# One core, attention into two expert layers: v rows for block means load into the place of the second batch's keys; norm's factor, key slices and the spread of w_out's conversion change with it

## The chip, the core and the metric

The kernel runs on one core of a Trainium2 chip. The metric is the time of one execution on the device in microseconds (us), median of the runs. Engines are named as in the profile: PE (TensorE), PEld (its weight loads), DVE (VectorE), ACT (ScalarE), POOL (GpSimd), SP (SyncE, which issues all DMAs here). L154 is line 154 of the kernel before.

## The reference

Attention with a local window and block summaries, then two feed-forward layers. Float32 throughout; the four weight matrices of the two layers arrive as float64.

```python
k_sum = k.reshape(B, H, nb, block, D).max(axis=3)      # B=2 H=8 S=768 D=64 block=32
v_sum = v.reshape(B, H, nb, block, D).mean(axis=3)
scores_l = scale * q @ k.T                             # only |i - j| < 16 kept
scores_s = scale * q @ k_sum.T + log(block)
a = softmax(concat(scores_l, scores_s))                # max subtracted
x = a @ concat(v, v_sum)                               # 1536 tokens x 512
h = x @ w_in                                           # 512 -> 1024
solu = h * softmax(h)
ln = (solu - mean) / sqrt(var + 1e-6) * g_ln
x = ln @ w_out                                         # 1024 -> 512
h = x @ w_in2                                          # 512 -> 2048
out = where(h > 0, h, exp(min(h, 0)) - 1) @ w_out2     # 2048 -> 512
```

## The kernel before, in words

**Attention.** The 1,536 tokens are cut into 24 units of 64 queries, 12 per batch. Unit n takes a window of 96 keys and the 24 block maxima of its batch: `attn_s` (L168) makes a tile kw of 120 keys by copying a slice of k_sb on POOL (L176) and, in the first units of a batch, the maxima ksum (L175), multiplies it with a block-diagonal q (s_ps, L179), masks on DVE (L185), takes exp on ACT (L188) and divides on POOL (L193). `attn_p` transposes the result (p_ps, L198), `attn_x` multiplies it with a tile vw of 96 rows of v and 24 block means (x_ps, L215); ACT writes the high part of xT (L218), DVE the remainder (L219, shown as L95). kw and vw have three buffers each, k_sb two places (one per batch), q four.

**Block means.** `sum_v` (L150) loads 768 rows of v in six DMAs (L154), and PE multiplies them with an averaging matrix (vs_ps, L156). The rows go into `v_rows`: parts of the tiles y1 and y2, which are free until the first layer's output is written. The same parts are `stage`, the places into which the 64-bit words of w_in are loaded: words 0 and 1 go into y0, 2 and 3 into the part of y1 where the v rows lie, 4 and 5 into y2, 6 and 7 into y0 again.

**Weights.** `convert` (L106) loads 512 KB of words (L107) and makes two float32 numbers of each float64, a high part and a remainder: ACT takes the absolute value (L113), POOL clamps (L114), DVE does three bit operations (L115 to L117), for w_out POOL multiplies with norm's factor g (L119), ACT copies the high part (L120), DVE subtracts (L121, shown as L95). Each product of the two layers is three matmuls on these parts (`mm3x`, L97 to L100).

**First layer.** Row tile j of 128 tokens needs units 2j and 2j+1. h is computed for two halves n of w_in, then `ffn1_ln` does the norm on DVE, ACT and POOL (L230 to L244), `ffn1_tr` transposes it on PE (t_ps, L254) and splits it into lnT on ACT and DVE (L256, L257), and `mm_out` multiplies three row tiles at once with w_out (y_ps). **Second layer.** Three blocks of 512 tokens, with w_in2 and w_out2 converted by `load_w3` and `load_w4` as the work goes on.

**What sets the order.** The order on SP is written by hand (`manual_schedule`, L352): a prologue (L354 to L384), then 24 ticks (L398), of which each loads, computes half a row tile of h, and does one step of the attention of units 3, 4 and 6 ticks ahead, with transposes (`after`), conversions (`converts`, L396) and w_in2 loads (L421) at fixed ticks. A DMA on SP waits for the DMA eight places earlier, and for the readers of the place into which it loads. The order of the other engines comes from the scheduler, and each engine works strictly in its order.

Of the kernel before, what the change touches and what calls it, by code (L numbers as in the profile page):

```python
# [9 lines left out]
F32 = mybir.dt.float32  # L10
# [4 lines left out]
AF = mybir.ActivationFunctionType  # L15
# [7 lines left out]
TQ = 64  # L23
# [11 lines left out]
NEG = -1.0e9  # L35
LEAD = 6
NBUF = 3
NG = 6


# [9 lines left out]
def tile_kernel(ctx: ExitStack, tc: tile.TileContext, qd, kT, v, w_in, w_out, g_ln, w_in2, w_out2,  # L50
# [10 lines left out]

    y = [com.tile([128, KD, TC], F32, name=f"y{i}") for i in range(NTOK // TC)]
    flat = [t.rearrange("p d s -> p (d s)") for t in y]
    rows = [[t[:, i * DM:(i + 1) * DM] for i in range(KD * TC // DM)] for t in flat]
    stage = [[t.bitcast(I32)[:, i * 1024:(i + 1) * 1024].rearrange("p (k f) -> p k f", k=KD)
              for i in range(KD * TC // 1024)] for t in flat]

# [14 lines left out]
    negh = p_ln.tile([128, 1], F32, name="negh")  # L82
    dump = p_ln.tile([128, F1], BF16, name="dump")
    mask = p_at.tile([128, 3, KW], F32, name="mask", bufs=1)
    kws = [p_at.tile([128, NP, KW], F32, name=f"kw{i}", bufs=1) for i in range(NBUF)]
    vws = [p_at.tile([128, DM], F32, name=f"vw{i}", bufs=1) for i in range(NBUF)]
    avg = p_at.tile([128, 128 + NB], F32, name="avg", bufs=1)
    nc.gpsimd.memset(negh, -0.5)
# [17 lines left out]
    def convert(bits, src, hi, lo, g=None):  # L106
        nc.sync.dma_start(bits, src if len(src.shape) == 3 else src.rearrange("p (k f) -> p k f", k=KD))  # L107
        words = bits.rearrange("p k (f two) -> p k f two", two=2)
        low, high = words[:, :, :, 0], words[:, :, :, 1]
        hi, lo = (t if len(t.shape) == 3 else t.rearrange("p (k f) -> p k f", k=KD) for t in (hi, lo))  # L110
        a = p_k.tile([128, KD, 128], I32, tag="conv", name="conv", bufs=3)
        x = a.bitcast(F32)
        nc.scalar.activation(x, high.bitcast(F32), AF.Abs)  # L113
        nc.gpsimd.tensor_scalar(x, x, F64_HUGE, F64_TINY, op0=ALU.min, op1=ALU.max)  # L114
        nc.vector.tensor_scalar(a, a, 3, 0x3FFFFFF8, op0=ALU.logical_shift_left, op1=ALU.bitwise_and)  # L115
        nc.vector.scalar_tensor_tensor(a, high, -0x40000000, a, op0=ALU.bitwise_and, op1=ALU.bitwise_or)
        nc.vector.scalar_tensor_tensor(a, low, 29, a, op0=ALU.logical_shift_right, op1=ALU.bitwise_or)  # L117
        if g is not None:
            nc.gpsimd.tensor_scalar(x, x, g, 0.0, op0=ALU.mult, op1=ALU.add)  # L119
        nc.scalar.activation(hi, x, AF.Copy)  # L120
        lo_of(lo, x, hi)  # L121

    early = stage[0] + stage[1] + stage[2]
    v_rows = rows[1] + rows[2]

    def load_w_in(n, k):
        cs = slice(n * 512, (n + 1) * 512)
# [21 lines left out]

    def sum_v(b):  # L150
        pst = psb.tile([128, DM], F32, tag="b", name="vs_ps")
        for i in range(S // 128):
            vt = v_rows[i]
            nc.sync.dma_start(vt, v[b, PAD + i * 128:PAD + (i + 1) * 128, :])  # L154
            c0 = NB - i * 4
            nc.tensor.matmul(pst, lhsT=avg[:, c0:c0 + 128], rhs=vt, start=i == 0, stop=i == S // 128 - 1)  # L156
        vsum[b] = p_at.tile([128, DM], F32, tag="vsum", name="vsum", bufs=1)
        nc.scalar.activation(vsum[b][WIN:KW, :], pst[WIN:KW, :], AF.Copy)
# [5 lines left out]
    def load_v(n):  # L164
        b, t = divmod(n, NT)
        nc.sync.dma_start(vws[n % NBUF][0:WIN, :], v[b, t * TQ:t * TQ + WIN, :])

    def attn_s(n):  # L168
        b, t = divmod(n, NT)
        j, half = divmod(n, 2)  # L170
        kw = kws[n % NBUF]
        if n not in q_bd:
            load_q(n)
        if t < NBUF and n:
            copy_pool(kw[:, :, WIN:KW], ksum[b])  # L175
        copy_pool(kw[:, :, 0:WIN], k_sb[b][:, :, t * TQ:t * TQ + WIN])  # L176
        sps = psb.tile([128, NP, 128], F32, tag="b", name="s_ps")
        for p in range(NP):
            nc.tensor.matmul(sps[:, p, 0:KW], lhsT=q_bd[n][:, p, :], rhs=kw[:, p, :], start=True, stop=True)  # L179
        sm = p_at.tile([128, NP, KW], F32, tag="sm", name="sm", bufs=NBUF)  # L180
        st = p_at.tile([128, 4, NP], F32, tag="st", name="st", bufs=NBUF)
        nm, ss, ri = (st[:, i, :] for i in range(3))
        mi = 1 if t == 0 else (2 if t == NT - 1 else 0)
        for p in range(NP):
            nc.vector.tensor_tensor_reduce(sm[:, p, :], sps[:, p, 0:KW], mask[:, mi, :], -scale, 3.0e38,  # L185
                                           op0=ALU.add, op1=ALU.min, accum_out=nm[:, p:p + 1])
        for p in range(NP):
            nc.scalar.activation(sm[:, p, :], sm[:, p, :], AF.Exp, bias=nm[:, p:p + 1], scale=-1.0,  # L188
                                 accum_out=ss[:, p:p + 1])
        nc.vector.tensor_scalar(ri, ss, 1e-9, None, op0=ALU.add)  # L190
        nc.vector.reciprocal(ri, ri)  # L191
        for p in range(NP):
            nc.gpsimd.tensor_scalar(sm[:, p, :], sm[:, p, :], ri[:, p:p + 1], 1.0, op0=ALU.mult, op1=ALU.mult)  # L193
        live[n] = sm
# [198 lines left out]
    for i, t in ((0, 11), (1, 17)):  # L393
        for d in range(KD):
            after[t + d].append((mm_out, i, d))
    converts = {3: 2, 4: 1, 6: 1, 9: 2, 10: 2}  # L396
    NU = B * NT
    for t, (j, n) in enumerate(ticks):  # L398
        s_n, p_n, x_n = t + LEAD, t + LEAD - 2, t + LEAD - 3
        if t == 0:  # L400
            sum_v(1)
        elif t == 1:
            load_k(1)
        elif t == 3:
            sum_k(1)
        if x_n < NU and t:
            load_v(x_n)
        if s_n < NU:
            for u in (s_n + 1, s_n):
                if u < NU and u not in q_bd:  # L410
                    load_q(u)
            attn_s(s_n)
        mm_in(j, n)
        if p_n < NU:
            attn_p(p_n)
        for f, *args in after[t]:
            f(*args)
        if x_n < NU:
            attn_x(x_n)
        more(converts.get(t, 0))  # L420
        if t in (13, 15, 17, 18, 19, 20, 21, 22):  # L421
            load_w3()
        if x_n == NU - 1:
            p_at.release()
            p_w3 = ctx.enter_context(tc.tile_pool(name="p_w3", bufs=1, side="left", reuse_waits="tile"))
            lnT_last = [p_w3.tile([128, KF1, TB], F32R, tag=f"lnT{c}", name="lnT") for c in range(2)]
# [35 lines left out]
             f == 0, f == KF2 - 1)  # L462

    def store(i, ops, t):
        o = rows[0][t]
        r0 = i * TC + t * 128
        if i == NTOK // TC - 1 and t == NTT - 1:
            for c in range(2):
                cs = slice(c * 256, (c + 1) * 256)
                if c:  # L470
                    nc.vector.tensor_copy(o[:, cs], ops[t][:, cs])
                else:
                    nc.scalar.activation(o[:, cs], ops[t][:, cs], AF.Copy)
                nc.sync.dma_start(out[r0:r0 + 128, cs], o[:, cs])
            return
        if t % 2:
            nc.vector.tensor_copy(o, ops[t])
        else:
            nc.scalar.activation(o, ops[t], AF.Copy)
        nc.sync.dma_start(out[r0:r0 + 128, :], o)  # L480
# [77 lines left out]
```

## Time and profile before

| | |
|---|---|
| median of 3 runs | 510.34 us (509.59 to 511.14) |
| profiled execution | 507.9 us |
| its span | 505.8 us |
| mean granted clock of PE | 0.993 |
| busy in the span | PE 96%, DVE 56%, ACT 52%, POOL 26% |

The shares are means over the whole span. PE's busy time counts matmuls at whatever clock they ran, and a matmul may wait inside a busy stretch, so the stages have to be read apart: in which of them does PE stand still, who releases it, and at what clock does it run behind that?

### The profile page before, as it was taken

The page shows a single profiled execution, that of the slowest core. Times are in us where ns is not written, and L with a number is a line of the kernel's source. Part 1 is how long each engine was busy: PE and PEld are TensorE (multiplying, and loading weights), DVE is VectorE, ACT ScalarE, POOL GpSimd, SP SyncE. Part 2 cuts the span into 40 slices and gives each one's busy share as a digit, 9 for nine tenths or more (in the row PEclk, how much of TensorE's full clock was granted, in tenths as well). Part 3 has the DMA queues.
Part 4 walks back from the last instruction along what each step waited for, and adds up shares of the span by engine and source line. Part 5 has one row for each costly group of instructions (what it writes and reads, how often), then busy time and mean ns, then how long its engine had stood idle before and what let it go on. Part 6 is the DMA issues. An engine that isn't in the chain of part 4 may idle for free.

```text
span 505.8 us, 7269 instructions
## 1 busy us (share of the span) xinstructions
PE 483.2 (96%) x2616; PEld 400.5 (79%) x2616; DVE 283.5 (56%) x680; ACT 261.8 (52%) x592; POOL 131.0 (26%) x216
## 2 busy tenths in 40 slices
PE   1789997999999999999999999999999999999997
PEld 1466876888988888999888888888888888888885
DVE  3689799798458747797999622351222235122222
ACT  1675896776568436655767433352323335232333
POOL 1867688688413321322232100000000000000000
PEclk9999998999999999999999999999999999999999
DMA  8989473171313400565454000020000002000002
GB/s 302 286 296 311 132 231 120 38 233 39 115 59 116 141 1 0 208 172 166 155 173 126 1 0 0 1 84 1 1 1 0 0 1 84 1 0 0 1 0 83
DMA packets 24563, 46.53 MB, mean 92 GB/s; under 512 B 2256, under 2 KB 11088, under 8 KB 24528
## 3 DMA queue, kind: packets, MB, share of 16 engines
q1 hardware_dynamic: 24528, 46.08, 28.6%
q8 instruction: 20, 0.33, 0.3%
q14 instruction: 15, 0.12, 0.1%
HBM read 42.93 MB, written 3.15 MB: 91 GB/s over the span
## 4 chain that ended last, share of the span: by engine, by line
PE 88%; DMA 3%; DVE 3%; ACT 2%; POOL 1%; issue 1%; SPq 1%; ACTq 0%; POOLq 0%
PE h L98 13%; PE h L100 13%; PE h L99 13%; PE o_ps L98 9%; PE o_ps L99 9%; PE o_ps L100 9%; PE y_ps L98 5%; PE y_ps L100 4%; PE s_ps L179 4%; PE y_ps L99 4%; PE x_ps L215 2%; DMA q_bd<-in_qd 2%; PE p_ps L198 2%; PE t_ps L254 1%; DMA k_sb<-in_kT 1%
## 5 line engine op out<-in xcount | busy, mean ns | idle before, releaser
L454 DVE SCALAR_TENSOR_TENSOR m<-m,h 128x512 f32<-128x512 f32 x48 | 32.9, 685 | 120.0 <-ACT m L453 119.8
L452 ACT ACTIVATE m<-h 128x512 f32<-128x512 f32 x48 | 28.7, 598 | 107.5 <-PE h L100 107.2
L99 PE MATMUL h<-y_hl,w 128*128 128x512 f32 x192 | 75.9, 395 | 0.0
L100 PE MATMUL h<-y_hl,w 128*128 128x512 f32 x192 | 75.9, 395 | 0.0
L98 PE MATMUL o_ps<-w,g_hl 128*128 128x512 f32 x192 | 75.5, 393 | 0.0
L99 PE MATMUL o_ps<-w,g_hl 128*128 128x512 f32 x192 | 75.4, 393 | 0.0
L98 PE MATMUL h<-y_hl,w 128*128 128x512 f32 x192 | 75.2, 395 | 0.0
L100 PE MATMUL o_ps<-w,g_hl 128*128 128x512 f32 x192 | 66.9, 392 | 0.0
L114 POOL TENSOR_SCALAR conv<-conv 128x512 f32<-128x512 f32 x48 | 36.4, 761 | 67.2 <-ACT conv L113 65.9
L193 POOL TENSOR_SCALAR sm<-sm,st 128x120 f32<-128x120 f32 x96 | 44.9, 484 | 16.7 <-DVE st L191 15.8
L95 DVE TENSOR_TENSOR g_hl<-m,g_hl 128x512 fp32r<-128x512 f32 x48 | 33.9, 707 | 24.4 <-ACT g_hl L455 24.4
L455 ACT ACTIVATE g_hl<-m 128x512 fp32r<-128x512 f32 x48 | 30.3, 630 | 32.5 <-DVE m L454 32.5
L179 PE MATMUL s_ps<-kw,q_bd 128*128 128x120 f32 x192 | 29.6, 301 | 15.9 <-DMA q_bd<-in_qd 13.3
L98 PE MATMUL y_ps<-lnT,w_out 128*128 128x384 f32 x128 | 44.0, 344 | 0.3 <-DVE lnT L95 0.2
L100 PE MATMUL y_ps<-lnT,w_out 128*128 128x384 f32 x128 | 43.1, 338 | 0.0
L99 PE MATMUL y_ps<-lnT,w_out 128*128 128x384 f32 x128 | 43.1, 336 | 0.0
L99 PEld LDWEIGHTS h<-y_hl,w 128*128 128x128 f32 x192 | 36.1, 188 | 8.6
L98 PEld LDWEIGHTS o_ps<-w,g_hl 128*128 128x128 f32 x192 | 36.1, 188 | 8.5
L100 PEld LDWEIGHTS h<-y_hl,w 128*128 128x128 f32 x192 | 36.1, 188 | 8.5
L98 PEld LDWEIGHTS h<-y_hl,w 128*128 128x128 f32 x192 | 36.1, 188 | 8.5
L100 PEld LDWEIGHTS o_ps<-w,g_hl 128*128 128x128 f32 x192 | 36.1, 188 | 8.2
L99 PEld LDWEIGHTS o_ps<-w,g_hl 128*128 128x128 f32 x192 | 36.1, 188 | 8.2
(77 smaller groups left out, 913.1 us busy)
## 6 DMA issues: line engine op xcount, KB each, us to landing
y<-in_w_in SPq DMA_DIRECT2D x20, 512.0 KB, 4.6
y<-in_w_out SPq DMA_DIRECT2D x16, 512.0 KB, 4.3
q_bd<-in_qd SPq DMA_DIRECT2D x24, 256.0 KB, 5.0
vw<-in_v SPq DMA_DIRECT2D x24, 192.0 KB, 4.2
bits<-in_w_out SPq DMA_DIRECT2D x8, 512.0 KB, 3.5
k_sb<-in_kT SPq DMA_DIRECT2D x8, 400.0 KB, 5.5
y<-in_v SPq DMA_DIRECT2D x12, 256.0 KB, 5.4
out<-y SPq DMA_DIRECT2D x11, 256.0 KB, 2.3
```

The costliest lines, as they stand in the source:

```text
L95: nc.vector.tensor_tensor(out_, x, hi.bitcast(F32), op=ALU.subtract)
L98: nc.tensor.matmul(ps, lhsT=l[0][ls], rhs=r[0][rs], start=first, stop=False)
L99: nc.tensor.matmul(ps, lhsT=l[0][ls], rhs=r[1][rs], start=False, stop=False)
L100: nc.tensor.matmul(ps, lhsT=l[1][ls], rhs=r[0][rs], start=False, stop=last)
L114: nc.gpsimd.tensor_scalar(x, x, F64_HUGE, F64_TINY, op0=ALU.min, op1=ALU.max)
L179: nc.tensor.matmul(sps[:, p, 0:KW], lhsT=q_bd[n][:, p, :], rhs=kw[:, p, :], start=True, stop=True)
L193: nc.gpsimd.tensor_scalar(sm[:, p, :], sm[:, p, :], ri[:, p:p + 1], 1.0, op0=ALU.mult, op1=ALU.mult)
L198: nc.tensor.transpose(pps[:KW, p, :], live[n][:, p, :], ident)
L215: nc.tensor.matmul(xps[ds, p, :], lhsT=vw[:KW, p * 128 + hh * D:p * 128 + (hh + 1) * D], rhs=pT[:KW, p, hh * TQ:(hh + 1) * TQ], start=True ...
L452: nc.scalar.activation(m, h2, AF.Relu, scale=-1.0)
L454: nc.vector.scalar_tensor_tensor(m, m, -1.0, h2, op0=ALU.add, op1=ALU.max)
L455: nc.scalar.activation(gh, m, AF.Copy)
```

## The change

- **v rows.** `sum_v` allocates a tile v_sb with tag "k" of pool p_k, which has two places. For batch 0 that is the place that k_sb of batch 1 will have. v_sb of batch 0, v_sb of batch 1 and then k_sb of batch 1 use it one after the other. y1 and y2 hold only words of weights until the first layer's output.
- **Norm's factor.** In `convert` for w_out, POOL's multiplication is gone. ACT's copy multiplies with g, and DVE computes x*g - hi in one operation.
- **Key slices.** kw has four buffers. Units 12 to 23 load their 96 keys from memory with a DMA of 192 KB (128 partitions, 4 pieces of 384 bytes), issued in the tick before; units 0 to 11 copy on POOL as before.
- **Spread of w_out's conversions.** One in each of the ticks 3 to 10, not 2, 1, 1, 2, 2 in the ticks 3, 4, 6, 9, 10. Seven w_in2 loads stand in the ticks of the first layer, not eight.

```diff
--- before.py
+++ after.py
@@ -35,6 +35,8 @@
 NEG = -1.0e9
 LEAD = 6
 NBUF = 3
+NKW = 4
+NCOPY = 12
 NG = 6
 
 
@@ -61,7 +63,7 @@
 
     y = [com.tile([128, KD, TC], F32, name=f"y{i}") for i in range(NTOK // TC)]
     flat = [t.rearrange("p d s -> p (d s)") for t in y]
-    rows = [[t[:, i * DM:(i + 1) * DM] for i in range(KD * TC // DM)] for t in flat]
+    rows = [t[:, i * DM:(i + 1) * DM] for t in flat[:1] for i in range(KD)]
     stage = [[t.bitcast(I32)[:, i * 1024:(i + 1) * 1024].rearrange("p (k f) -> p k f", k=KD)
               for i in range(KD * TC // 1024)] for t in flat]
 
@@ -82,7 +84,7 @@
     negh = p_ln.tile([128, 1], F32, name="negh")
     dump = p_ln.tile([128, F1], BF16, name="dump")
     mask = p_at.tile([128, 3, KW], F32, name="mask", bufs=1)
-    kws = [p_at.tile([128, NP, KW], F32, name=f"kw{i}", bufs=1) for i in range(NBUF)]
+    kws = [p_at.tile([128, NP, KW], F32, name=f"kw{i}", bufs=1) for i in range(NKW)]
     vws = [p_at.tile([128, DM], F32, name=f"vw{i}", bufs=1) for i in range(NBUF)]
     avg = p_at.tile([128, 128 + NB], F32, name="avg", bufs=1)
     nc.gpsimd.memset(negh, -0.5)
@@ -115,13 +117,14 @@
         nc.vector.tensor_scalar(a, a, 3, 0x3FFFFFF8, op0=ALU.logical_shift_left, op1=ALU.bitwise_and)
         nc.vector.scalar_tensor_tensor(a, high, -0x40000000, a, op0=ALU.bitwise_and, op1=ALU.bitwise_or)
         nc.vector.scalar_tensor_tensor(a, low, 29, a, op0=ALU.logical_shift_right, op1=ALU.bitwise_or)
-        if g is not None:
-            nc.gpsimd.tensor_scalar(x, x, g, 0.0, op0=ALU.mult, op1=ALU.add)
-        nc.scalar.activation(hi, x, AF.Copy)
-        lo_of(lo, x, hi)
+        if g is None:
+            nc.scalar.activation(hi, x, AF.Copy)
+            lo_of(lo, x, hi)
+        else:
+            nc.scalar.activation(hi, x, AF.Copy, scale=g)
+            nc.vector.scalar_tensor_tensor(lo, x, g, hi.bitcast(F32), op0=ALU.mult, op1=ALU.subtract)
 
     early = stage[0] + stage[1] + stage[2]
-    v_rows = rows[1] + rows[2]
 
     def load_w_in(n, k):
         cs = slice(n * 512, (n + 1) * 512)
@@ -149,8 +152,9 @@
 
     def sum_v(b):
         pst = psb.tile([128, DM], F32, tag="b", name="vs_ps")
+        v_sb = p_k.tile([128, NP, S + 2 * PAD], F32, tag="k", name="v_sb", bufs=2).rearrange("p a s -> p (a s)")
         for i in range(S // 128):
-            vt = v_rows[i]
+            vt = v_sb[:, i * DM:(i + 1) * DM]
             nc.sync.dma_start(vt, v[b, PAD + i * 128:PAD + (i + 1) * 128, :])
             c0 = NB - i * 4
             nc.tensor.matmul(pst, lhsT=avg[:, c0:c0 + 128], rhs=vt, start=i == 0, stop=i == S // 128 - 1)
@@ -165,15 +169,22 @@
         b, t = divmod(n, NT)
         nc.sync.dma_start(vws[n % NBUF][0:WIN, :], v[b, t * TQ:t * TQ + WIN, :])
 
+    def load_kw(n):
+        b, t = divmod(n, NT)
+        if NCOPY <= n < B * NT:
+            nc.sync.dma_start(kws[n % NKW][:, :, 0:WIN],
+                              kT[b, :, :, t * TQ:t * TQ + WIN].rearrange("p d s -> d p s"))
+
     def attn_s(n):
         b, t = divmod(n, NT)
         j, half = divmod(n, 2)
-        kw = kws[n % NBUF]
+        kw = kws[n % NKW]
         if n not in q_bd:
             load_q(n)
-        if t < NBUF and n:
+        if t < NKW and n:
             copy_pool(kw[:, :, WIN:KW], ksum[b])
-        copy_pool(kw[:, :, 0:WIN], k_sb[b][:, :, t * TQ:t * TQ + WIN])
+        if n < NCOPY:
+            copy_pool(kw[:, :, 0:WIN], k_sb[b][:, :, t * TQ:t * TQ + WIN])
         sps = psb.tile([128, NP, 128], F32, tag="b", name="s_ps")
         for p in range(NP):
             nc.tensor.matmul(sps[:, p, 0:KW], lhsT=q_bd[n][:, p, :], rhs=kw[:, p, :], start=True, stop=True)
@@ -393,7 +404,7 @@
     for i, t in ((0, 11), (1, 17)):
         for d in range(KD):
             after[t + d].append((mm_out, i, d))
-    converts = {3: 2, 4: 1, 6: 1, 9: 2, 10: 2}
+    converts = {3: 1, 4: 1, 5: 1, 6: 1, 7: 1, 8: 1, 9: 1, 10: 1}
     NU = B * NT
     for t, (j, n) in enumerate(ticks):
         s_n, p_n, x_n = t + LEAD, t + LEAD - 2, t + LEAD - 3
@@ -409,6 +420,7 @@
             for u in (s_n + 1, s_n):
                 if u < NU and u not in q_bd:
                     load_q(u)
+            load_kw(s_n + 1)
             attn_s(s_n)
         mm_in(j, n)
         if p_n < NU:
@@ -418,7 +430,7 @@
         if x_n < NU:
             attn_x(x_n)
         more(converts.get(t, 0))
-        if t in (13, 15, 17, 18, 19, 20, 21, 22):
+        if t in (13, 15, 19, 20, 21, 22, 23):
             load_w3()
         if x_n == NU - 1:
             p_at.release()
@@ -462,7 +474,7 @@
              f == 0, f == KF2 - 1)
 
     def store(i, ops, t):
-        o = rows[0][t]
+        o = rows[t]
         r0 = i * TC + t * 128
         if i == NTOK // TC - 1 and t == NTT - 1:
             for c in range(2):
```

The order moves at three places of which the prediction speaks. The rows of the change have the changed kernel's own line numbers: its L109 is L107 of before, L143 L140, L158 L154, L166 L162, L170 L166, L97 L95, L118 and L119 are L116 and L117, L125 is the new operation. "waits" names the queues and engines of which the instruction waits (DMAHW0 to 7: the DMA that last went through that one of eight queues).

SP in the prologue, from the fifth row of v (y2, y1: places of words) to the vw load behind q of unit 2, before:

```order
L154 DMA y2_67<-in_v 128x512 [waits DMAHW0_49]
L154 DMA y2_67<-in_v 128x512 [waits DMAHW1_49]
L107 DMA y1_66<-in_w_in 128x1024 [waits DMAHW4_49,DMAHW5_49,DMAHW2_49,PE_49]
L107 DMA y1_66<-in_w_in 128x1024 [waits DMAHW6_49,DMAHW7_49,DMAHW3_49,PE_49]
L162 DMA q_bd_236<-in_qd 128x512
L166 DMA vw1_103<-in_v 96x512
```

and with the change:

```order
L158 DMA v_sb_191<-in_v 128x512 [waits DMAHW0_49]
L158 DMA v_sb_191<-in_v 128x512 [waits DMAHW1_49]
L109 DMA y1_66<-in_w_in 128x1024 [waits DMAHW2_49]
L109 DMA y1_66<-in_w_in 128x1024 [waits DMAHW3_49]
L166 DMA q_bd_238<-in_qd 128x512 [waits DMAHW4_49]
L170 DMA vw1_104<-in_v 96x512 [waits DMAHW5_49]
```

The two w_in loads wait for two or three DMAs and PE in one case, and for one DMA each in the other.

SP at the second batch's keys, from the last row of v, before:

```order
L154 DMA y2_67<-in_v 128x512 [waits DMAHW5_49]
L162 DMA q_bd_442<-in_qd 128x512 [waits DMAHW6_49]
L162 DMA q_bd_444<-in_qd 128x512 [waits DMAHW7_49,PE_49]
L140 DMA k_sb_499<-in_kT 128x800 [waits DMAHW0_49]
L140 DMA k_sb_499<-in_kT 128x800 [waits DMAHW1_49]
```

and with the change:

```order
L158 DMA v_sb_431<-in_v 128x512 [waits DMAHW5_49]
L166 DMA q_bd_446<-in_qd 128x512 [waits DMAHW6_49]
L166 DMA q_bd_448<-in_qd 128x512 [waits DMAHW7_49,PE_49]
L143 DMA k_sb_503<-in_kT 128x800 [waits DMAHW3_49,DMAHW2_49,DMAHW4_49,DMAHW1_49,DMAHW5_49,DMAHW0_49,PE_49]
L143 DMA k_sb_503<-in_kT 128x800 x3
L170 DMA vw1_104<-in_v 96x512
```

The first k_sb load waits for the v rows and for PE; the loads behind it follow.

DVE at the first transposes of the norm (t_ps to lnT; ln, st: the next row tile's norm; conv, w_out: conversions), before:

```order
L95 TENSOR_TENSOR lnT_94<-t_ps_904,lnT_93 128x4x128 [waits Activation_49]
L116 SCALAR_TENSOR_TENSOR conv_944<-y0_65,conv_944 128x512 [waits DMAHW3_49,DVE_49]
L237 SCALAR_TENSOR_TENSOR ln_993,st_991<-h_884,ln_993 128x1024 [waits Activation_49]
L239 TENSOR_SCALAR st_991<-st_991 128x1
L117 SCALAR_TENSOR_TENSOR conv_944<-y0_65,conv_944 128x512 [waits DVE_49]
L95 TENSOR_TENSOR lnT_94<-t_ps_911,lnT_93 128x4x128 [waits Activation_49]
L95 TENSOR_TENSOR w_out_87<-conv_780,w_out_87 128x512 [waits Activation_49]
L240 TENSOR_TENSOR st_991<-st_991 128x1 [waits DVE_49]
L95 TENSOR_TENSOR lnT_94<-t_ps_918,lnT_93 128x4x128 [waits Activation_49]
L95 TENSOR_TENSOR lnT_94<-t_ps_925,lnT_93 128x4x128 [waits Activation_49]
```

and with the change:

```order
L97 TENSOR_TENSOR lnT_94<-t_ps_906,lnT_93 128x4x128 [waits Activation_49]
L125 SCALAR_TENSOR_TENSOR w_out_87<-conv_852,gT_95,w_out_87 128x512 [waits Activation_49]
L245 TENSOR_REDUCE st_992<-h_886 128x1 [waits PE_49]
L254 SCALAR_TENSOR_TENSOR st_819<-st_819 128x1 [waits Pool_49]
L97 TENSOR_TENSOR lnT_94<-t_ps_913,lnT_93 128x4x128 [waits Activation_49]
L97 TENSOR_TENSOR lnT_94<-t_ps_920,lnT_93 128x4x128 [waits Activation_49]
L125 SCALAR_TENSOR_TENSOR w_out_88<-conv_946,gT_95,w_out_88 128x512 [waits Activation_49]
L97 TENSOR_TENSOR lnT_94<-t_ps_927,lnT_93 128x4x128 [waits Activation_49]
L97 TENSOR_TENSOR xT_839<-x_ps_934,xT_838 128x4x64 [waits Activation_49]
L248 SCALAR_TENSOR_TENSOR ln_994,st_992<-h_886,ln_994 128x1024 [waits Activation_49]
```

Of the second row tile's norm (ln) and the conversion steps, what stood between the first and the second lnT stands behind the fourth or ahead of the first, and the remainder of a w_out stands between the first and second and between the third and fourth.

## Rows read from the trace of the kernel before

**Rows 1.** Page, part 1: busy us, share of the span, instructions of each engine.

```profile
PE 483.2 (96%) x2616; PEld 400.5 (79%) x2616; DVE 283.5 (56%) x680; ACT 261.8 (52%) x592; POOL 131.0 (26%) x216
```

**Rows 2.** Waits of PE, whole run: what was waited for, us, times, longest.

```profile
PE s_ps L179 <- DMA q_bd<-in_qd: 13.3, 2, 10.9
PE s_ps L179 <- DVE lnT L95: 2.4, 1, 2.4
...
PE h L99 <- DMA y<-in_v: 0.6, 1, 0.6
```

**Rows 3.** Chain of waits, 18 to 62 us: start, us, what.

```profile
18.43 5.69 DMA q_bd<-in_qd
...
24.26 2.03 PE s_ps L179 x8
...
27.97 1.10 PE s_ps L179 x8
...
39.26 5.32 DMA k_sb<-in_kT
...
60.60 0.44 PE p_ps L198 x4
61.04 0.61 PE x_ps L215 x16
```

**Rows 4.** Timeline of PE: start, us, engine, line, operation, times, idle before.

```profile
20.47 1.34 PE L198 MATMUL p_ps<-ident,sm 128*120 128x128 f32 x4 [0.28 <-POOL sm L193]
...
43.54 1.02 PE L156 MATMUL vs_ps<-y,avg 128*128 128x512 f32 x2
...
46.19 0.45 PE L215 MATMUL x_ps<-pT,vw 120*64 120x64 f32 x8
...
48.12 1.15 PE L179 MATMUL s_ps<-kw,q_bd 128*128 128x120 f32 x8
...
73.03 1.04 PE L179 MATMUL s_ps<-kw,q_bd 128*128 128x120 f32 x8
```

**Rows 5.** Windows: busy us of PE, PEld, DVE, ACT, POOL; PEclk, DMA share, GB/s.

```profile
16.00:18.00 2.00, 2.00 (x6) 0.89 (x5) 1.93 (x5) 1.46 (x7) 1.90 (x4) 1.00 0.56 170
24.00:26.00 2.00, 1.74 (x8) 1.77 (x8) 0.02 (x1) 0.63 (x2) 1.73 (x3) 0.54 1.09 294
60.00:70.00 10.00, 10.00 (x82) 8.32 (x81) 10.00 (x45) 9.54 (x33) 5.79 (x12) 1.00 0.53 148
86.00:88.00 2.00, 2.00 (x9) 1.69 (x9) 2.00 (x12) 0.00 (x0) 1.39 (x2) 0.50 0.90 348
```

**Rows 6.** Chain of waits, 81 to 86 us.

```profile
81.63 0.68 DVE conv L116
82.31 1.14 DVE ln L237 x2
...
83.52 0.70 DVE conv L117
...
84.87 1.43 PE s_ps L179 x8
```

**Rows 7.** Page, part 6: issues, KB each, median us to landing.

```profile
vw<-in_v SPq DMA_DIRECT2D x24, 192.0 KB, 4.2
...
y<-in_v SPq DMA_DIRECT2D x12, 256.0 KB, 5.4
```

**Rows 8.** Timeline of SP, DMA issues: 8.9 us, and q of unit 12.

```profile
8.91 3.47 SPq L154 DMA_DIRECT2D y<-in_v  x6
...
64.20 0.41 SPq L162 DMA_DIRECT2D q_bd<-in_qd  x1
```

**Rows 9.** Groups by line: busy us, mean ns, idle before.

```profile
L454 DVE SCALAR_TENSOR_TENSOR m<-m,h 128x512 f32<-128x512 f32 x48 | 32.9, 685 | 120.0 <-ACT m L453 119.8
...
L95 DVE TENSOR_TENSOR w_out<-conv,w_out 128x512 fp32r<-128x512 f32 x8 | 6.2, 772 | 0.1
...
L119 POOL TENSOR_SCALAR conv<-conv,gT 128x512 f32<-128x512 f32 x8 | 5.5, 693 | 2.0 <-DVE conv L117 2.0
```

## The prediction, made before the changed kernel had run

> **What bounds the kernel now.** I read the busy times first: TensorE (PE) is busy 483.2 of 505.8 us [rows 1]. A gain must therefore come out of stretches in which PE stands still or runs slowly. The waits of PE name those stretches: two waits for q_bd (10.9 us at the start, 2.4 us later), one of 2.4 us for lnT, one of 0.6 us for a row of v, and hardly anything else [rows 2]. The chain of waits then tells what ends the second q_bd wait: that load is issued at 18.43, takes 5.69 us, and the scores of unit 2 start at 24.26 [rows 3]. PE had finished the transposes of unit 1 at 20.47 + 1.34 = 21.8 [rows 4]. The windows show two further things. From 16 to 18 the DMA engines moved 170 GB/s at a share of 0.56, so they had room just when SP stood still ahead of that load; and the granted clock is 0.54 from 24 to 26 and 0.50 from 86 to 88 [rows 5], the lower level (1.2 of 2.4 GHz), each time right behind an idle stretch of 2.4 us. So every 2.4 us wait is paid for twice.
>
> DVE is the second resource. From 60 to 70 it is busy for all 10.00 us [rows 5]; PE can run ahead of it only as far as its buffers reach.
>
> **A. First v rows into the place of the second k_sb: -3.7 us.** Before, words 3 and 4 of w_in took the places that the matmuls of vs had just read, so SP stood still until PE had done those matmuls, and q of unit 2 is queued behind. Now nothing but DMA landings holds SP. The sixth v row is issued at about 12.4, the two w_in loads and q follow as the loads eight places earlier land; the first v row, issued at 8.91, lands after about 5.4 us [rows 7], which puts the issue of q near 14.8, not 18.43. The two w_in loads and q, 1,280 KB, then fill the gap at 16 to 18. With the 5.69 us of before q lands at 20.5; even with 7.0 it is there when PE is free at 21.8. The wait goes: 24.26 - 21.8 = -2.45. The scores took 2.03 us at the low clock, and the next unit's 1.10 at the high one [rows 3]: -0.9. The x_ps matmuls behind them ran at the low clock too, for which I take -0.35. Sum -3.7. If PE now waits for the vsum copies on POOL instead, the clock falls anyway: -2.4. The most is -4.1.
>
> **B. Second v rows: -0.5.** They waited for DVE to finish converting the words in whose place they went; the wait of 0.6 us at the first h matmuls [rows 2] has its cause in such a place. Between 0 and -0.6.
>
> **C. The second k_sb behind the last vs matmul: +1.0.** This is the new wait. Before, those four loads were issued at 39.26 and took 5.32 us to the first reduction [rows 3], and the chain runs through them. Now the first must wait until PE has read the last v row, and the loads of vw, q and w_out are queued behind it on SP. The last pair of vs matmuls began at 43.54 and took 1.02 us [rows 4]: 44.56. With A and B in hand I put that at about 40.3, so the loads land at 44.5 to 45.6, no earlier than before, while the rest of the work is 4 us ahead. DVE runs in order: behind the first two ksum reductions stand a unit's masks and an xT remainder, for which PE's next h matmuls wait. PE has h matmuls of the running tile to go on with; I take 1.0, nearer to the waits under 1 us of rows 2 than to the whole lead. Bounds: 0 and +4.0 (the lead given back).
>
> **D. The order of PE at 46 to 48 us: -0.8.** Transposes and x_ps matmuls alternated one by one from 46.19 to 48.12, 1.93 us [rows 4], where 0.44 + 0.61 = 1.05 is what they take in groups [rows 3]. In the new order they mostly stand in groups. Between 0 and -0.9.
>
> **E. The first transposes of ln: -3.0.** Scores of unit 13 waited 2.4 us for lnT. Ahead of that remainder DVE did two steps of a conversion and an LN product, 0.68 + 1.14 + 0.70 = 2.52 us [rows 6]. With the even spread of w_out, DVE does the lnT remainders first, and PE's new order has 10 h matmuls between the third and the fourth group of transposes. What can go is the wait and the clock behind it: 1.43 - 1.10 = 0.33 on the scores [rows 3, 6] and half of the 2 us from 86 to 88 [rows 5], together 2.4 + 1.3 = 3.7. I leave 0.7 as a new wait, since a w_out remainder of 0.77 us [rows 9] still stands between the lnT ones. Bounds: 0 and -3.7.
>
> **F. Waits that I don't see: +1.0.** A kernel with PE 6 us ahead meets DVE, full at 60 to 70 [rows 5], and w_out loads that are due sooner. Bounds 0 and +2.4, the longest of rows 2 behind the first.
>
> **Nothing for the rest.** The factor of norm leaves POOL (eight times 693 ns [rows 9]) and goes into a copy on ACT and a two-operation remainder on DVE; that form takes 685 ns for 128x512, the subtraction 772 [rows 9], so DVE doesn't grow. POOL has no entry among PE's long waits. The 12 copies of key slices leave POOL too. In their place 12 DMAs of 192 KB go to SP, one unit ahead, right behind q of that unit: q of unit 12 is issued at 64.20 [rows 8], its scores start at 73.03 [rows 4], 8.8 us later, and a vw load of the same 192 KB lands in 4.2 [rows 7]. Even at twice that the slice is there in time, so I take 0; the bound is 0 to +24, 12 slices each 2 us late, for which the load would have to take 10.8 us. A slice has rows of 384 bytes, where a vw row has 2,048. The page "DMA: Bandwidth & Descriptors" of the Trainium skill, under Specifications, says that pieces under 512 bytes miss the line rate, because the engine reads, modifies and writes; no run here shows the price, and by it an estimate is a load twice as long, 8.4 us, still inside 8.8. One w3 conversion moves into the last stage. Behind 90 us PE waits for nothing that counts [rows 2], so it is hidden; without that cover it costs about five operations of 0.7 us.
>
> **Sum.** -3.7 - 0.5 + 1.0 - 0.8 - 3.0 + 1.0 = -6.0. The profiled execution took 507.9 us (505.8 of span, 2.1 around it), so it should become 501.9. It is 2.4 below the median of the three runs, 510.34; the median should become 504.3.
>
> **Rivals.**
> *DVE absorbs it.* PE's lead is eaten at 60 to 70, where DVE has no room, and DVE's own end doesn't move, because its ksum reductions come no earlier (C at its bound). Then A, B and D bring about 5 and C takes 4 of it; E brings some 1.5 more: -2.5, 507.8. For it: 10.00 of 10 busy. Against: the first loads also feed DVE earlier, and it was idle for the first DMA waits.
>
> *The second k_sb comes late, and the kernel is slower.* PE's order has transposes between the vs matmuls, and these wait for POOL's sm. If that keeps the last vs matmul at 44.56, k_sb is there at 44.6 + 5.3 = 49.9, 5.3 later than now. DVE is held in order, PE runs out of h matmuls after, say, 1.5 us and stands still for 3.8; the clock falls as behind the other long waits, 1.3 more (E). The lead of A and B is used up by the waits of the transposes, D stays, E's wait comes as before: 3.8 + 1.3 - 0.8 = +4.3, 514.6. With E's 3.0 gained it is slower only if less than 1.3 us of the lead is left at the last vs matmul, so from 43.3 on. For it: the chain already goes through that load. Against: v rows no longer wait for conversions.
>
> *The key slices are slow.* Twelve late slices of up to 2 us: +24 at the most, less the 6: about 520. The rule of the skill named above points this way; the 8.8 us of room point against it.
>
> *The loads were not what q waited for.* If the DMA engines are as full in the new order, q lands at 24 all the same, and C and F are left without A: within 1 us of 510.3.
>
> **How the numbers follow.** Forecast (-3.5 to -9.5): 0.60. DVE absorbs it (-1.5 to -3.5): 0.20. No change: 0.07. k_sb late: 0.09. Slices slow: 0.04. A measurement of this kernel tells about 0.3% from no change, 1.5 us: faster is below 508.8, slower above 511.9. Faster: 0.60 + 0.20 = 0.80; same 0.07; slower 0.13. All gains at their bounds and no new wait give -4.1 - 0.6 - 0.9 - 3.7 = -9.3, 501.0; the low end is 500.0 for reorderings not costed. All against gives -2.4 + 4.0 + 2.4 = +4.0, 514.3. The range stops at 510.0: it holds the forecast, the absorbed case and half of no change, and leaves out the two slower ones.
>
> **What would show it.** A: no wait for q_bd behind the first, the second scores near 22, the clock at 1.0 from 24 to 28, SP's w_in loads without a wait for vs_ps. C: k_sb issued near 40 and a DVE wait for it; later than 43.3 means the slower case. E: no wait of over 1 us for lnT, the clock at 1.0 at the first transposes. Key slices: no PE or weight-load wait for kw from DMA. The forecast is wrong if PE's lead at unit 12's scores is under 2 us, or if a new wait of over 2 us stands among PE's.

## The result, and the profile after

| | before | changed |
|---|---|---|
| median | 510.40 us (4 runs, 509.59 to 511.14) | 505.72 us (4 runs, 505.23 to 505.84) |
| profiled execution | 507.9 us, span 505.8 | 505.2 us, span 503.5 |

The ratio is 0.9903 (95% interval 0.9889 to 0.9917): 4.7 us faster. Forecast were 504.3, between 500.0 and 510.0. On a second chip the same two kernels gave 0.9914 (0.9895 to 0.9933).

The page and the waits of PE of the changed kernel (answering to [rows 1, 2]; L190 is L179 of before, L102 L100, L209 L198, L229 L218):

```profile
PE 479.6 (95%) x2616; PEld 397.5 (79%) x2616; DVE 288.5 (57%) x680; ACT 263.2 (52%) x592; POOL 120.8 (24%) x198
```

```profile
PE s_ps L190 <- DMA q_bd<-in_qd: 12.3, 1, 12.3
PE s_ps L190 <- issue: 1.7, 1, 1.7
PE p_ps L209 <- POOL sm L204: 1.6, 4, 0.5
PE h L102 <- DVE xT L97: 1.2, 2, 0.7
PE s_ps L190 <- ACT vsum L162: 0.9, 1, 0.9
...
PE x_ps L226 <- POOL vw L93: 0.7, 2, 0.4
PE h L101 <- DVE w_in L97: 0.6, 1, 0.6
```

One wait for q_bd is left, the first, and the wait of 2.4 us for lnT has become one of 1.7. The view puts that one down to "issue", that is, it names nothing that released it; DVE's second lnT remainder, the first of the two in the row of 82.40 below, ends at 83.08, and the scores of unit 13 start at 83.18, so I read it as the wait for lnT again. Behind them stand more small waits than before.

```profile
81.12 1.21 DVE L245 TENSOR_REDUCE st<-h 128x1 f32<-128x1024 f32 x1
...
82.40 1.27 DVE L97 TENSOR_TENSOR lnT<-t_ps,lnT 128x512 fp32r<-128x512 f32 x2
```

The first wait differs by chance: 12.3 us here, 10.9 before [rows 2]. It is the landing of the first q, whose instructions ahead are the same in both kernels; in the profiled executions of the twelve experiments the first scores start between 10.8 and 12.4, with the v rows in either place (11.6 in experiment 4, which has the old place, and 10.8 in experiment 11, which has the new one). So the two traces are compared from their first scores, and all leads below are counted from there: before at 10.86 us, here at 12.26.

The timeline of PE, answering to [rows 3, 4]:

```profile
12.26 3.44 PE L190 MATMUL s_ps<-kw,q_bd 128*128 128x120 f32 x16 [12.26 <-DMA q_bd<-in_qd]
...
23.47 1.06 PE L190 MATMUL s_ps<-kw,q_bd 128*128 128x120 f32 x8
...
40.32 2.74 PE L160 MATMUL vs_ps<-v_sb,avg 128*128 128x512 f32 x6
...
47.58 1.15 PE L190 MATMUL s_ps<-kw,q_bd 128*128 128x120 f32 x8 [0.87 <-ACT vsum L162]
...
72.55 1.05 PE L190 MATMUL s_ps<-kw,q_bd 128*128 128x120 f32 x8
...
83.18 1.12 PE L190 MATMUL s_ps<-kw,q_bd 128*128 128x120 f32 x8 [1.66 <-issue]
```

Second scores: 24.26 - 10.86 = 13.40 before, 23.47 - 12.26 = 11.21 here, a lead of 2.2 us. End of the last vs matmul: 44.56 before, 40.32 + 2.74 = 43.06 here, a lead of 2.9. Scores of unit 12 (73.03 and 72.55): 1.9. Scores of unit 13 (84.87 and 83.18): 3.1. The ends of the spans (505.8 and 503.5): 3.7. The medians show 4.7; this one execution of before was quick in more than its start.

The windows, answering to [rows 5]:

```profile
16.00:18.00 2.00, 2.00 (x6) 0.80 (x6) 2.00 (x12) 2.00 (x10) 1.34 (x3) 1.00 1.07 403
24.00:26.00 2.00, 1.25 (x23) 0.93 (x22) 1.97 (x9) 0.97 (x4) 1.80 (x3) 1.00 1.04 328
60.00:70.00 10.00, 9.79 (x79) 7.92 (x78) 8.41 (x37) 9.30 (x34) 7.95 (x14) 1.00 0.79 234
86.00:88.00 2.00, 2.00 (x9) 1.65 (x10) 2.00 (x12) 1.37 (x3) 0.61 (x1) 1.00 0.43 105
```

DMA moves 403 GB/s from 16 to 18, where it moved 170, and the granted clock stays at its upper level (2.4 GHz) in all four.

SP's DMA issues: w_in words 2 and 3, q of unit 2, and the second batch's keys; then SP's longest single wait from 8 to 60 us, which is for the last vs matmul:

```profile
13.80 1.46 SPq L109 DMA_DIRECT2D y<-in_w_in  x2
15.62 0.33 SPq L166 DMA_DIRECT2D q_bd<-in_qd  x1
...
43.09 1.75 SPq L143 DMA_DIRECT2D k_sb<-in_kT  x4
```

```profile
SPq L143 <- PE vs_ps L160: 5.3, 1, 5.3
```

q of unit 2 is issued at 15.62, 2.8 us earlier, or 4.2 counted from the first scores; it takes 7.5 us to land, and its scores start at 23.47, some 0.3 us behind the landing. The keys go out at 43.09, 3.8 later than the 39.26 of before [rows 3], or 2.4 counted from the first scores.

### The profile page after: what moved, and what is told of

Read it like the earlier page. It is cut to its first block, busy times and chain, and to the rows that moved or that the text cites. A ratio compares the mean times of both kernels' runs of the same rounds, so it can differ in the third digit from the quotient of the medians.

```text
span 503.5 us, 7265 instructions
## 1 busy us (share of the span) xinstructions
PE 479.6 (95%) x2616; PEld 397.5 (79%) x2616; DVE 288.5 (57%) x680; ACT 263.2 (52%) x592; POOL 120.8 (24%) x198
## 4 chain that ended last, share of the span: by engine, by line
PE 85%; DVE 8%; POOL 2%; ACT 1%; DMA 1%; issue 1%; SPq 1%; POOLq 0%; ACTq 0%
PE h L100 12%; PE h L102 12%; PE h L101 12%; PE o_ps L100 9%; PE o_ps L101 9%; PE o_ps L102 9%; PE y_ps L102 4%; PE y_ps L101 4%; PE y_ps L100 4%; PE s_ps L190 3%; PE x_ps L226 2%; PE t_ps L265 2%; DVE sm L196 2%; DMA q_bd<-in_qd 1%; PE p_ps L209 1%; POOL sm L204 1%
## 5 line engine op out<-in xcount | busy, mean ns | idle before, releaser
L102 PE MATMUL h<-y_hl,w 128*128 128x512 f32 x192 | 75.9, 395 | 0.0
L100 PE MATMUL o_ps<-w,g_hl 128*128 128x512 f32 x192 | 75.6, 394 | 0.0
L100 PE MATMUL h<-y_hl,w 128*128 128x512 f32 x192 | 75.2, 395 | 0.0
L102 PE MATMUL o_ps<-w,g_hl 128*128 128x512 f32 x192 | 66.9, 392 | 0.0
L116 POOL TENSOR_SCALAR conv<-conv 128x512 f32<-128x512 f32 x48 | 36.3, 757 | 76.9 <-ACT conv L115 75.8
L204 POOL TENSOR_SCALAR sm<-sm,st 128x120 f32<-128x120 f32 x96 | 47.1, 508 | 31.3 <-DVE st L202 26.3
L97 DVE TENSOR_TENSOR g_hl<-m,g_hl 128x512 fp32r<-128x512 f32 x48 | 33.1, 690 | 24.4 <-ACT g_hl L467 24.4
L100 PE MATMUL y_ps<-lnT,w_out 128*128 128x384 f32 x128 | 43.5, 341 | 0.0
L102 PE MATMUL y_ps<-lnT,w_out 128*128 128x384 f32 x128 | 43.1, 336 | 0.0
L100 PEld LDWEIGHTS o_ps<-w,g_hl 128*128 128x128 f32 x192 | 36.1, 188 | 8.6
L100 PEld LDWEIGHTS h<-y_hl,w 128*128 128x128 f32 x192 | 36.1, 188 | 8.5
L102 PEld LDWEIGHTS h<-y_hl,w 128*128 128x128 f32 x192 | 36.1, 188 | 8.5
L102 PEld LDWEIGHTS o_ps<-w,g_hl 128*128 128x128 f32 x192 | 36.1, 188 | 8.3
L190 PE MATMUL s_ps<-kw,q_bd 128*128 128x120 f32 x192 | 28.2, 293 | 15.1 <-DMA q_bd<-in_qd 12.3
```

The lines of the kernel that those rows point to most:

```text
L97: nc.vector.tensor_tensor(out_, x, hi.bitcast(F32), op=ALU.subtract)
L100: nc.tensor.matmul(ps, lhsT=l[0][ls], rhs=r[0][rs], start=first, stop=False)
L102: nc.tensor.matmul(ps, lhsT=l[1][ls], rhs=r[0][rs], start=False, stop=last)
```

## The experiments

Diffs are against the kernel named. Differences in us are taken from the ratio of the runs to those of before on the same chip. All leads are counted from the first scores of the same trace, since that start varies.

**1. The v rows alone (against before).**

```diff
-            vt = v_rows[i]
+            vt = v_sb[:, i * DM:(i + 1) * DM]      # v_sb: tag "k" of p_k, as in the change
```

> Before with the v rows in the place of the second k_sb and nothing else. My theory: A, B and C belong to this part, E to the spread of w_out, so -2.5 to -3.5 us of the 4.7 measured; the wait for q of unit 2 is gone, k_sb is issued near 43, the wait for lnT at the first transposes stays at 2 to 2.5 us with the clock at half behind it. Rival (the whole gain is the v rows'): -4 to -5, and the wait for lnT goes too, because PE's order at the transposes changes with it (its order has h matmuls between the groups of transposes).

509.20 us against 510.24, ratio 0.9986 (0.9967 to 1.0005): 0.7 us, and not clear of zero, far less than either theory gave. The lead is there early (second scores without a wait for q), is 3.0 at the scores of unit 13, 1.0 at those of unit 16, and 0.6 at the end of the span. The waits of PE, and of ACT from 60 to 130 us:

```profile
PE s_ps L179 <- DMA q_bd<-in_qd: 12.3, 1, 12.3
PE h L100 <- DVE xT L95: 1.7, 3, 0.9
PE s_ps L179 <- ACT pT L200: 1.5, 1, 1.5
...
PE s_ps L179 <- DVE lnT L95: 0.6, 1, 0.6
```

```profile
ACT w_out L120 <- POOL conv L119: 3.0, 2, 2.7
```

The wait for lnT has gone from 2.4 to 0.6 without the spread, as the rival had it: with the v rows moved the scheduler no longer puts the norm's product ln (1.14 us) between the first two lnT remainders of DVE. Elsewhere PE waits more, for xT (1.7) and for pT on ACT (1.5). ACT waits 3.0 us for norm's factor on POOL, but 2.7 of them at 106 to 109 us, behind the stretch in which the lead falls to 1.0.

**2. All but the v rows (against the change).**

```diff
-            vt = v_sb[:, i * DM:(i + 1) * DM]
+            vt = v_rows[i]                         # parts of y1 and y2, as before
```

> The changed kernel with the v rows in the places of words again. My theory: the wait of 2.4 us for q of unit 2 and its half clock are back, the first transposes stay good, so -1 to -2 against before. Rival (the whole gain is the v rows'): within 1 us of before. Second rival (the key slices, factor and spread cost something that v pays for): slower than before by 1 or more.

508.41 us, 0.9974 (0.9954 to 0.9993): 1.3 us, inside what my theory gave. The wait for q of unit 2 is back with 3.0 us. So the rest brings 1.3 alone, v 0.7 alone, and both together over 4.

**3. Only the first batch's v rows in the new place (against the change).**

```diff
+            vt = v_rows[i] if b else v_sb[:, i * DM:(i + 1) * DM]
```

> The changed kernel, but only the first batch's v rows in the place of the second k_sb; the second batch's rows go into the places of words as before, and k_sb no longer waits for the second vs matmuls. If that wait (C) gives back 1 us or more between 45 and 57 us of the span, and the wait for words (B) is worth only 0.5, this is 0.5 to 1.5 us faster than the changed kernel (504.2 to 505.2). If what is given back there is DVE's own load and not the wait, it is the same as the changed kernel or up to 1 us slower, since the v rows wait for conversions again.

507.28 us, 0.9951 (0.9926 to 0.9977) against 0.9903: slower, not faster. The keys go out at 38.05, 5 us earlier. The chain of waits and the windows:

```profile
38.05 5.32 DMA k_sb<-in_kT
...
46.75 1.72 DVE ksum L149 x2
48.47 0.61 DVE conv L119
...
49.10 0.64 ACT w_in L121
...
49.78 0.79 PE h L100
```

```profile
48.00:50.00 2.00, 0.22 (x1) 0.22 (x1) 2.00 (x11) 0.90 (x3) 0.47 (x1) 0.91 1.01 263
50.00:52.00 2.00, 2.00 (x7) 1.37 (x7) 1.40 (x10) 1.98 (x10) 0.00 (x0) 0.50 0.86 271
```

The keys land early, and the ksum reductions stand in DVE's order ahead of the last steps of a w_in conversion. PE waits for that conversion's copy on ACT (L121) until 49.78, idle for 1.9 us, and the clock falls to 0.50. The vs matmuls begin at 36.76 here and at 36.71 in the changed kernel: the second v rows came in time in both, so what they wait for is worth nothing (B). In the changed kernel the reductions come after:

```profile
48.36 1.81 DVE L148 TENSOR_REDUCE ksum<-k_sb 128x24 f32<-128x768 f32 x2
```

The wait that the change adds thus keeps the keys' reductions (1.81 us for two of the four; the other two stand later still) out of the stretch in which DVE still converts w_in.

**4. The spread alone (against before).**

```diff
-    converts = {3: 2, 4: 1, 6: 1, 9: 2, 10: 2}
+    converts = {3: 1, 4: 1, 5: 1, 6: 1, 7: 1, 8: 1, 9: 1, 10: 1}
-        if t in (13, 15, 17, 18, 19, 20, 21, 22):
+        if t in (13, 15, 19, 20, 21, 22, 23):
```

> Before with w_out's conversions at one a tick and one w_in2 load fewer in the first layer, and nothing else. My theory (E is the spread's): the wait for lnT falls under 1 us and the clock stays up, -2 to -3 us. Rival (the wait hangs on DVE's order at the transposes, which the spread alone leaves as it was): the wait for lnT stays at 2.4, within 0.7 us of before.

513.62 us, 1.0072 (1.0044 to 1.0099): 3.7 us slower.

```profile
PE s_ps L179 <- DVE lnT L95: 2.4, 1, 2.4
PE p_ps L198 <- DVE lnT L95: 1.3, 1, 1.3
```

The wait for lnT is as it was, 2.4, and a second one of 1.3 has come at the transposes after. My attribution of E falls.

**5. Keys one tick later (against the change).**

```diff
-        elif t == 1:
+        elif t == 2:
             load_k(1)
-        elif t == 3:
+        elif t == 4:
             sum_k(1)
```

> The changed kernel with the load of the second batch's keys and its block maxima one tick later (load in tick 2, maxima in tick 4). Theory (the place of the ksum reductions in DVE's order decides what PE loses between 45 and 57 us of the span; the earlier run with them earlier lost 3.4 us there): they now stand behind the conversions of w_in and the masks, PE gives back less than the 1.4 us of the changed kernel there, so the same to 1.5 us faster than the changed kernel (504 to 506 on a chip where before takes 510.3). Rival (the late load is the cost): the maxima come late for units 12 and 13, PE waits at 73 us, slower than the changed kernel by 1 or more.

504.97 us, 0.9899 (0.9874 to 0.9925): the same as the changed kernel within the intervals. Once the reductions stand behind the conversions, more delay buys nothing that shows.

**6 to 8. The change without one part each: spread, key slices, factor.**

```diff
-    converts = {3: 1, 4: 1, 5: 1, 6: 1, 7: 1, 8: 1, 9: 1, 10: 1}    # 6, with the w_in2 ticks
+    converts = {3: 2, 4: 1, 6: 1, 9: 2, 10: 2}
-            load_kw(s_n + 1)                                        # 7, with three buffers
-        if n < NCOPY:
-            copy_pool(kw[:, :, 0:WIN], k_sb[b][:, :, t * TQ:t * TQ + WIN])
+        copy_pool(kw[:, :, 0:WIN], k_sb[b][:, :, t * TQ:t * TQ + WIN])
-            nc.scalar.activation(hi, x, AF.Copy, scale=g)           # 8
-            nc.vector.scalar_tensor_tensor(lo, x, g, hi.bitcast(F32), op0=ALU.mult, op1=ALU.subtract)
+            nc.gpsimd.tensor_scalar(x, x, g, 0.0, op0=ALU.mult, op1=ALU.add)
+            nc.scalar.activation(hi, x, AF.Copy)
+            lo_of(lo, x, hi)
```

> The changed kernel with w_out's conversions in the ticks 3, 3, 4, 6, 9, 9, 10, 10 and eight w_in2 loads in the first layer, as before. The spread alone cost 3.7 us. Theory (the spread is bad by itself but good behind a PE that runs ahead, because it evens DVE's load from 60 to 130): 1 to 2.5 us slower than the changed kernel. Rival (the spread costs here too): 1 to 3 us faster than the changed kernel, near 503.

> The changed kernel with three kw buffers and POOL copies for all 24 units. Theory of the prediction (slices are worth nothing): within 0.7 us of the changed kernel. Rival (POOL is on the path at 60 to 130, since the v rows alone gained 3 us by 40 and lost them by 110): 1.5 to 3 us slower than the changed kernel, with longer waits of PE for sm on POOL.

> The changed kernel with norm's factor as a multiplication on POOL again. Theory of the prediction (worth nothing): within 0.7 us of the changed kernel. Rival (the step on POOL between DVE and ACT lengthens each of the eight conversions by 0.7 us and more, and DVE and ACT stand behind it in order): 1 to 3 us slower.

Without the spread 505.19 us, 0.9919 (0.9886 to 0.9951); without the slices 507.03, 0.9938 (0.9916 to 0.9959); without the factor 508.77, 0.9982 (0.9968 to 0.9996), all against before at 509.73. So the factor is worth most, 3.5 to 4 us in company of the others; the slices 1.8 by the first ratio of the change and 1.2 by the second, with intervals that touch; the spread nothing that can be told. The part that I had put at nothing is the one without which most of the gain goes.

Waits of PE, then of ACT from 60 to 130 us, without the factor; then rows of its timelines of PE and ACT:

```profile
PE h L100 <- ACT xT L227: 2.5, 3, 1.7
```

```profile
ACT w_out L122 <- POOL conv L121: 1.2, 2, 0.9
```

```profile
85.62 1.70 PE L188 MATMUL s_ps<-kw,q_bd 128*128 128x120 f32 x8
```

```profile
79.96 0.69 ACT L115 ACTIVATE conv<-y 128x512 f32<-128x512 f32 x1 [1.36 <-DMA y<-in_w_out]
...
83.11 1.56 ACT L265 ACTIVATE lnT<-t_ps 128x512 fp32r<-128x512 f32 x3
84.55 0.41 ACT L227 ACTIVATE xT<-x_ps 128x256 fp32r<-128x256 f32 x1
...
92.44 0.63 ACT L122 ACTIVATE w_out<-conv 128x512 fp32r<-128x512 f32 x1 [0.92 <-POOL conv L121]
```

ACT waits for POOL's multiplication here, and not in the changed kernel. But that wait does not show how the factor costs PE its time. The scores of unit 13 start 73.8 us behind the first scores here (85.62 against 11.83), where the changed kernel has 70.9, so most of the loss is there before ACT's first wait for POOL, which ends at 92.44. What PE waits for ahead of unit 13 is a copy of xT that stands on ACT behind three copies of lnT, and what ACT had last waited for is a landing of w_out's words. On DVE the norm's product ln stands between the first two lnT remainders once more, as in the kernel before. So the factor's worth is shown; that it comes from the other order that the scheduler makes without POOL's step, and not from a wait for POOL, is what these rows suggest, and the path stays open.

The profiled execution without the spread was that kernel's slowest, 508.7, and shows where the old spread is touchy. The chain of waits, and the windows:

```profile
50.09 9.20 DMA y<-in_w_out
```

```profile
64.00:66.00 2.00, 2.00 (x10) 1.90 (x10) 1.91 (x8) 2.00 (x6) 0.27 (x1) 0.50 0.00 0
```

The first of two w_out loads that it issues behind the late keys and six loads of vw and q took 9.20 us to land, the second as long; ACT stood at the first in order, PE's waits added up and the clock fell to 0.50. With one conversion in tick 3 that load took from 50.40 to about 57.4, where ACT begins, and there is no second. Four of its five runs took 504.5 to 505.7, so this time is the exception. Experiment 11 has the old spread too, and in its profiled execution, also that kernel's slowest (507.85), the same load took 9.0 us. One trace of each does not show that the landing makes the difference.

**9. Six places for w_out's words (against the change).**

```diff
-        convert(early[k % 2], w_out[...
+        convert(early[(k + 2) % 6], w_out[...
```

> The changed kernel, and w_out's words go in turn through all six places (which the v rows have left), not through two. Theory (what is left at 60 to 110 us of the span is ACT standing in order at a w_out landing, because SP waits with each load until the words two before are converted, 20.9 us on SP): the loads go out earlier, ACT no longer waits for y<-in_w_out for more than 1 us in all (3.9 now), PE's waits at 80 to 88 shrink from 2.3 to under 1.5; 1 to 2.5 us faster than the changed kernel. Rival (DVE itself is full there, 9.6, 10.0 and 10.0 of 10 us from 70 to 100): the same within 0.7.

508.56 us, 0.9969 (0.9952 to 0.9986), slower than the changed kernel at 505.56 on the same chip. SP's waits from 55 to 112 us, here and in the changed kernel of experiment 12, and ACT's here:

```profile
SPq L170 <- PE x_ps L226: 38.9, 10, 9.8
```

```profile
SPq L109 <- DVE conv L119: 20.5, 4, 7.8
SPq L170 <- PE x_ps L226: 17.4, 8, 6.3
```

```profile
ACT conv L115 <- DMA y<-in_w_out: 4.0, 4, 1.7
```

The third w_out load on SP, here and in the changed kernel:

```profile
60.97 0.41 SPq L109 DMA_DIRECT2D y<-in_w_out  x1
```

```profile
65.03 0.34 SPq L109 DMA_DIRECT2D y<-in_w_out  x1
```

The 20.5 us for conversions are gone from SP, and the wait for x_ps (a vw place, earlier in the same queue) has grown from 17.4 to 38.9. The first half of the theory holds: the third to the seventh load leave 4 to 8 us earlier. The second half falls: ACT still waits 4.0 us for landings (4.5 in the changed kernel of that chip), PE's waits from 80 to 88 are 3.3 us and not under 1.5, and the kernel is 3.0 us slower. The profiled execution was the fastest of this kernel's twelve (506.74), so its trace need not show where the time goes; why this order is worse is open.

**10. Six places and the keys one tick later.**

> The run before with the second batch's keys one tick later as well. If the two add: 0 to 1 us faster than the six places alone, near 503. If DVE is the bound in both, the same as the better of the two.

505.99 us, 0.9920 (0.9898 to 0.9942): as the changed kernel. The two don't add.

**11. v rows and factor (against before; the diffs of 1 and 8).**

> Before with two parts of the change, v rows and norm's factor, and neither slices nor spread. v alone gained 0.7, everything but the factor 1.0. Theory (v gives the lead, and the factor on POOL is what loses it at 60 to 110): 2.5 to 4 us faster than before, since slices took 1.8 of 4.7 and the spread little. Rival (it needs all parts): under 1.5 us.

506.92 us, 0.9941 (0.9923 to 0.9960): 3.0 us faster, where v alone gives 0.7. These two together carry most of the change. The factor alone was not run.

**12. The changed kernel again, same chip as 9 to 11.**

> The changed kernel unaltered, on the same chip as the three others: 4.7 us faster than before, give or take 1, as measured first.

505.56 against 509.77, 0.9914 (0.9895 to 0.9933).

## Why the prediction was right, and where its steps were not

- **A held, smaller.** Forecast -3.7; the lead is 2.2 at the second scores and 2.9 at the end of the vs matmuls. The wait for q and the low clock are gone as said, but narrowly: q was issued near where I put it and then took 7.5 us to land, where I had 5.69 and at most 7.0, and landed some 0.3 us ahead of its scores. What I had left as a bound came in part: PE waits 0.7 us for the vsum copies on POOL. Experiment 2 brings the wait back with 3.0 us.
- **B was 0, not -0.5**: another wait (w_in on DVE) stands in the same place, and the vs matmuls start the same with either place of the rows (experiment 3).
- **C was wrong in its mechanism.** The lead falls from 2.9 to 1.9 between 44 and 73 us, so C and D together cost 1.0, where I had 0.2. The last vs matmul ended at 43.06, which is 41.7 if the first scores are put at the 10.86 of before: 1.4 later than the 40.3 that I gave, by what A and B fell short, and 1.6 earlier than the 43.3 of the slower case. That case's cause did not come: PE has no wait between the vs matmuls, and sm on POOL holds it only 0.5 us ahead of them, in both kernels. And the late keys did not hold DVE: the reductions stand later in its order, and it has no wait for the keys. Taking the wait away cost time (experiment 3), so "the new wait" was a price I had with the wrong sign.
- **D came as said and was given back**: transposes and x_ps stand in groups, and the scores behind them wait 0.9 us for a vsum copy on ACT.
- **E had the right place and the wrong cause.** The wait fell from 2.4 to 1.7, and the clock stays up; the lead grows by 1.2 from unit 12 to 13, where I had 3.0. I had left a w_out remainder between the lnT remainders; the maximum of the next row tile (L245, 1.21 us) stands there too, as the rows of the order already showed. It is not the spread: alone it leaves the wait at 2.4 and costs 3.7 us (experiment 4), while the v rows alone take it to 0.6 (experiment 1).
- **"Nothing for the rest" is the step that failed.** I priced POOL's multiplication by POOL's absence among PE's waits, at 0. Without the factor's move hardly 1 us of the gain is left: it is worth 3.5 to 4 us in company of the others (experiment 8). A list of PE's waits does not price such a step: with it the orders of DVE and ACT differ too. The path from there to PE stays open. Nor was DVE's new operation as cheap as the nearest row: 950 ns on average in the changed kernel (806 in experiment 7), where L454 takes 685 and the subtraction took 772 [rows 9]. Two of the eight make that average, with 1.30 and 1.56 us; the other six take 0.74 to 0.88. ACT's copy with a factor takes 723, without it 635.

```profile
L125 DVE SCALAR_TENSOR_TENSOR w_out<-conv,gT,w_out 128x512 fp32r<-128x512 f32 x8 | 7.6, 950 | 0.2 <-ACT w_out L124 0.2
...
L124 ACT ACTIVATE w_out<-conv,gT 128x512 fp32r<-128x512 f32 x8 | 5.8, 723 | 0.2 <-DVE conv L119 0.2
```

```profile
83.60 1.30 DVE L125 SCALAR_TENSOR_TENSOR w_out<-conv,gT,w_out 128x512 fp32r<-128x512 f32 x1
...
91.36 1.56 DVE L125 SCALAR_TENSOR_TENSOR w_out<-conv,gT,w_out 128x512 fp32r<-128x512 f32 x1
```

- **The key slices were in time**, at no price on DMA: they land in 4.8 us, a vw load of the same size in 4.3 of the same trace (4.2 before [rows 7]). The Trainium skill ("DMA: Bandwidth & Descriptors", Specifications) says that pieces under 512 bytes miss the line rate. The load twice as long that I had estimated by that is not seen in this trace, with pieces of 384 bytes. Whether the copies that POOL was spared count is not settled: 1.2 to 1.8 us, with intervals that touch (experiment 7).

```profile
vw<-in_v SPq DMA_DIRECT2D x24, 192.0 KB, 4.3
...
kw<-in_kT SPq DMA_DIRECT2D x12, 192.0 KB, 4.8
```

- **The sum** came near (505.7 against 504.3): A, E and C with D each brought less or cost more than I had, and F, put at 1.0, did not come as a loss behind unit 13, where the lead grew by another 0.6 to the end; DVE is busy for 8.41 of the 10 us from 60 to 70, not full. In the pair of traces the steps make 3.7, where I had 6.0. The total rests on v rows and factor together, which I did not see, so that it came out near is in part luck. The parts don't add: 0.7 (v) and 1.3 (the rest) make 4.2 to 4.7.
- **By its own signs** the forecast was at the edge. PE's lead at the scores of unit 12 was to be at least 2 us and is 1.9 (0.5 if the starts are not put together), and the wait for lnT was to be at most 1 us and is 1.7. No new wait of over 2 us stands among PE's, no wait for kw from DMA, and SP's w_in loads have no wait for vs_ps.

## What to carry to other kernels

A lead that one engine wins early need not last: the v rows alone were 3.0 us ahead at unit 13 and 0.6 at the end, and gained 0.7; with the factor moved as well the gain is 3.0. So price a part of a change in company of the others, not against the old schedule. An engine that is missing in the bottleneck's list of waits is not thereby free: a step taken off POOL was worth 3.5 to 4 us here, though no wait of PE names it, and ACT's two waits for it, 1.2 us in all, come when most of the time is lost already. And align two traces at the first piece of work before reading any difference: here the start alone varied by 1.5 us.

## What the runs showed of the hardware that was not expected

- A wait taken from an in-order DMA queue can return under another name: 20.5 us for conversions became 21.5 us more for x_ps, and though five loads left 4 to 8 us earlier, the kernel was slower (experiment 9).
- The same two-operation form of DVE on 128x512 takes 685 ns with one operand in PSUM (L454), and with all operands and a factor per partition in SBUF 0.74 to 0.88 us in six of eight times here and 1.30 and 1.56 in the other two. Both long ones run while POOL does its product ln (L255, 1.19 us); in experiment 7 one beside the same product took 0.75. Whether that is the cause was not tried.
- Two loads of 512 KB issued behind four loads of keys and six of vw and q took 9.2 us each to land (experiment 6), against 7.0 for the one load that the changed kernel has in that place and a median of 4.3 for w_out's words before.
